# Score matmuls of an attention and gated-MLP block in runs of 16, with a new order of all steps

## The chip, the cores and the metric

The kernel runs on one core of a Trainium2 chip. The metric is the device time of one execution in microseconds (us), as a median over several executions. Four engines compute: TensorE (PE) multiplies matrices into eight PSUM banks, VectorE (DVE) and ScalarE (ACT) work on elements, and GpSimd (POOL) here only prepares constants and issues some DMAs. SyncE (SP) issues most of the other DMAs.

## The reference, cut to what matters

The input x has 2048 rows of 512 elements, in bfloat16. The first half is attention with 32 heads of 16 elements, in which each row sees 8 earlier rows, 2 apart. The second half is a gated MLP of width 1376.

```python
q, k, v = split_heads(layernorm(x) @ wqkv)        # 32 heads of 16
idx = pos[:, None] - arange(8)[None, :] * 2       # 8 shifts: 0, 2, ..., 14
logits = einsum("bhsd,bhswd->bhsw", q, k[idx]) * 16 ** -0.5
logits = where(idx >= 0, logits, -1e9)
o = einsum("bhsw,bhswd->bhsd", softmax(logits), v[idx])
h = x + merge_heads(o) @ wo
n = layernorm(h)
return h + (relu(n @ W_gate) * (n @ W_up)) @ W_down
```

## The kernel before

**Chunks.** The 2048 rows are worked on in 4 chunks (`tk`) of 512 rows; a chunk is 4 blocks (`j`) of 128 rows. The 512 columns are 4 tiles (`t`) of 128. Lines are those of the kernel before.

**First norm and QKV.** `layernorm` takes the statistics on DVE (bn_stats, L393, and bn_aggr, L396), ACT works out 1/sqrt by Ln and Exp (L406, L410), and DVE writes the normalized row (L428). PE transposes it (L459), and a copy (L473 on ACT, for two blocks of chunk 0 L471 on DVE) puts it into a `quad` tile. Twelve groups of four matmuls (L505) per chunk make q, k and v in transposed form; ACT copies each group out of its bank (L513).

**Scores.** The 8 shifts are two halves (`hf`) of four. For a half, DVE multiplies q by four shifted views of k (L552), for two tiles t at a time: two products of 128 x 4096 per half, each in a `big` tile. PE then sums over the elements of a head with the constant matrix `sel` (L558). Such a matmul has 32 output rows, and four of them with different `tile_position` fill the 128 rows of one bank. A product gives 8 matmuls, and a half has two products, which add up in the same bank. ACT takes the exp of the bank (L574); in chunk 0 a mask follows (L577).

**Softmax sum and values.** L591 sums the two halves' exps, ACT makes the reciprocal by Ln and Exp (L594, L597). In chunks 1 to 3 the exps are scaled by it (L606); in chunk 0 the scaling comes at the end (L647). PE spreads each shift's weights over the head's rows with matmuls on 32 rows of the array (L619), and ACT copies the 8 banks into one `big` tile (L625). For each t DVE multiplies by the 8 shifted views of v (L640) and adds the shifts up: the first addition, of halves of 4 shifts, is a DMA with accumulation issued by POOL (L672) in chunks 0 to 2 and a DVE add in chunk 3; the rest are DVE adds (L643, L666).

**Output of attention and MLP.** L692 multiplies by wo, L703 adds the residual on DVE and sums the row, L363 on ACT gives the sum of squares of the second norm, which ends as the first does. The MLP goes by 11 groups of 128 columns: up and gate (L730), copies out by ACT (L734, L737), product on DVE (L750). L767 multiplies by W_down, L778 adds the residual on DVE, and L782 on SP stores the result.

**Order.** Every step is an `Op` with an engine, an estimated duration, the steps that it depends on, buffers and a priority. `Plan.order` places the steps one after the other: of the steps that can start soonest on an engine, it takes the one with the lowest `prio`, and it gives out the buffers too (8 PSUM `bank`s, 9 `quad`, 5 `big`, 5 `row`, 2 `up_sb`, 2 `gr` and others). The priority comes from the list `RANK`, by the number of the step in the order of creation. The order that results is written into the program, and each engine works through its own queue of instructions in that order. `MERGE` is the tuple of chunks whose score matmuls of one half make one step. `DMAT` names norms that are transposed by DMA, `LNA` those whose normalized row is written on ACT; the first is empty, the second all zeros.

Of the kernel before, what the change touches and what calls it, by code (L numbers as in the profile page):

```python
# [8 lines left out]
P = 128  # L9
# [6 lines left out]


RANK = [
    0, 1, 2, 3, 4, 5, 6, 7, 8, 9, 10, 11, 12, 13, 14, 15, 18, 17, 19, 22,
    25, 30, 34, 37, 27, 32, 38, 21, 24, 28, 31, 33, 36, 40, 16, 20, 23, 26, 29, 35,  # L20
    39, 42, 44, 48, 53, 43, 51, 56, 41, 62, 67, 54, 55, 64, 77, 84, 46, 50, 65, 71,
    73, 76, 89, 92, 93, 97, 75, 79, 69, 74, 85, 99, 96, 119, 123, 128, 72, 94, 82, 102,
    105, 108, 141, 154, 158, 135, 147, 139, 153, 143, 116, 130, 120, 126, 134, 165, 175, 213, 215, 219,
    157, 167, 199, 217, 238, 174, 185, 230, 234, 240, 184, 194, 227, 233, 236, 245, 250, 243, 247, 248,
    254, 251, 258, 261, 265, 253, 255, 262, 268, 263, 270, 274, 277, 281, 288, 285, 291, 293, 287, 292,
    282, 294, 296, 310, 318, 319, 326, 302, 306, 330, 335, 346, 325, 352, 334, 337, 342, 354, 307, 328,
    362, 313, 321, 361, 365, 316, 323, 338, 369, 373, 353, 374, 355, 358, 344, 372, 336, 350, 378, 371,
    377, 357, 382, 380, 387, 349, 379, 390, 363, 388, 375, 385, 366, 408, 417, 421, 424, 437, 442, 467,
    472, 419, 495, 498, 501, 384, 429, 470, 476, 52, 59, 47, 60, 45, 57, 49, 58, 63, 70, 83,
    91, 81, 88, 95, 80, 86, 78, 87, 90, 107, 117, 100, 103, 104, 109, 98, 101, 136, 151, 166,  # L30
    173, 127, 137, 131, 171, 155, 168, 152, 156, 163, 169, 122, 132, 129, 203, 150, 216, 222, 149, 221,
    160, 235, 241, 246, 249, 252, 257, 298, 266, 278, 283, 275, 272, 305, 308, 314, 311, 312, 339, 347,
    376, 381, 317, 327, 356, 359, 324, 333, 360, 368, 332, 340, 364, 370, 392, 399, 389, 393, 401, 406,
    404, 410, 403, 407, 398, 402, 409, 412, 413, 416, 420, 423, 426, 433, 430, 436, 439, 428, 431, 432,
    435, 438, 473, 480, 481, 496, 461, 468, 488, 499, 502, 448, 451, 444, 449, 443, 445, 453, 457, 459,
    465, 471, 456, 464, 458, 463, 486, 489, 493, 505, 414, 477, 483, 490, 394, 450, 455, 511, 497, 523,
    520, 540, 500, 515, 546, 550, 553, 492, 504, 503, 506, 508, 541, 562, 573, 576, 538, 564, 578, 583,
    531, 567, 575, 580, 548, 565, 587, 590, 66, 110, 68, 111, 106, 112, 61, 113, 115, 133, 145, 162,
    138, 144, 164, 140, 146, 142, 159, 161, 170, 176, 212, 220, 172, 178, 204, 207, 177, 180, 195, 201,
    218, 224, 200, 205, 182, 189, 179, 186, 191, 197, 188, 192, 242, 271, 284, 297, 320, 264, 289, 295,  # L40
    299, 304, 341, 343, 345, 383, 348, 415, 425, 422, 418, 427, 391, 395, 411, 400, 396, 434, 441, 462,
    466, 452, 460, 491, 494, 440, 447, 474, 478, 446, 454, 485, 487, 512, 518, 516, 524, 509, 514, 528,
    532, 521, 542, 527, 539, 522, 526, 535, 536, 544, 545, 549, 555, 551, 557, 560, 556, 561, 554, 558,
    563, 568, 569, 577, 584, 591, 595, 571, 574, 597, 598, 604, 618, 622, 621, 624, 596, 619, 626, 627,
    633, 606, 610, 623, 628, 593, 600, 642, 609, 613, 582, 588, 586, 592, 602, 607, 617, 645, 650, 637,
    643, 616, 620, 612, 630, 652, 547, 572, 552, 579, 585, 660, 665, 668, 672, 654, 674, 678, 681, 661,
    669, 673, 676, 648, 671, 675, 679, 114, 124, 118, 148, 125, 183, 121, 181, 187, 190, 198, 206, 193,
    208, 210, 196, 211, 202, 209, 214, 225, 229, 223, 226, 259, 280, 267, 290, 239, 244, 231, 237, 228,
    232, 276, 286, 256, 260, 273, 301, 269, 303, 279, 315, 309, 300, 322, 329, 331, 351, 386, 367, 397,
    405, 469, 475, 479, 482, 484, 507, 513, 519, 510, 517, 525, 533, 534, 530, 529, 566, 608, 611, 614,  # L50
    543, 570, 581, 601, 537, 594, 599, 603, 559, 589, 605, 615, 631, 636, 641, 647, 635, 639, 625, 629,
    638, 640, 649, 651, 644, 646, 632, 634, 653, 655, 657, 664, 658, 663, 666, 659, 667, 656, 662, 670,
    713, 718, 694, 699, 716, 720, 711, 715, 723, 709, 712, 701, 705, 687, 707, 708, 710, 714, 685, 688,
    689, 691, 696, 700, 680, 684, 703, 690, 693, 692, 695, 683, 686, 677, 682, 697, 698, 702, 704, 717,
    719, 724, 706, 721, 727, 725, 729, 722, 726, 730, 733, 739, 744, 749, 731, 735, 738, 743, 728, 734,
    736, 740, 742, 746, 747, 748, 732, 737, 741, 745,
]


# [33 lines left out]
class Plan:  # L93
# [9 lines left out]
    def add(self, key, *a, **k):  # L103
        op = Op(*a, **k)
        op.key = key
        op.seq = len(self.ops)
        if RANK:
            op.prio = RANK[op.seq]
        self.ops.append(op)
        for b in set(op.take) | set(op.use):  # L110
            b.left += 1
        return op
# [57 lines left out]
def kernel(  # L170
# [11 lines left out]
    nc = tc.nc  # L182
# [4 lines left out]
    NT = D // P  # L187
# [116 lines left out]
    add = plan.add  # L304
# [3 lines left out]

    DACC = tuple((k, t) for k in range(3) for t in range(4))
    DAL = 5.5  # L310
    NWARM = 48
    DMAT = ()

# [1 line left out]

    RPE, OPE = (), ()

    MERGE = ()

    BCN = 4  # L320

# [18 lines left out]
    def layernorm(tk, src, dst_slots, pr, groups, on_act, residual=None):  # L340
        ln = "h" if residual else "x"


        dst = Buf(dst_slots)
        mv, rs, nb = Buf(mv_s), Buf(rs_s), Buf(nb_s)
        sm, sq = (residual, Buf(sq_s)) if residual else (None, None)
        evs = []
        for grp in groups:
            ag, xns = [], {}
            gk = str(grp[0]) if len(groups) > 1 else ""  # L350
            lo, hi = grp[0], grp[-1] + 1
            for j in grp:
                if residual:
# [8 lines left out]
                    def f_sq(j=j, xn=xns[j], h=h):  # L362
# [4 lines left out]
                    a = add((ln + "nm" + gk, tk), "DVE", DSM, f_nm, [src[j][0]], pr, take=[mv], use=[sm], lat=DL)  # L367
                    ag.append(add((ln + "sq" + gk, tk), "ACT", A5 + 0.1 if h else 0.73, f_sq, [a], pr,
                                  take=[sq, xns[j]], use=[mv] + ([h] if h else []), lat=AL))
                elif tk == 0 and j == BPC - 1:  # L370
# [15 lines left out]
                    a = add(("xsu", tk), "ACT", 0.75, f_su, [src[j]], pr, take=[xns[j], sm], lat=AL)  # L386
                    a = add(("xnm", tk), "DVE", DSM, f_nm, [a], pr, take=[mv], use=[sm], lat=DL)
                    ag.append(add(("xsq", tk), "ACT", 0.75, f_sq, [a], pr, use=[mv, xns[j]], lat=AL))
                else:
# [8 lines left out]
                    a = add((ln + "st" + gk, tk), "DVE", DST, f_st, [src[j]], pr, take=[st], lat=DL)  # L398
# [40 lines left out]
            if (ln, tk) in DMAT:  # L439
                for j in range(lo, hi):  # L440
                    xn, a = norm(j)

                    def f_td(j=j, xn=xn):
                        for t in range(NT):
                            nc.sync.dma_start_transpose(out=dst.t[:, t, j * P:(j + 1) * P],
                                                        in_=xn.t[:, t * P:(t + 1) * P])

                    evs.append(add((ln + "td" + gk, tk), "SP", 2.0, f_td, [a], pr, take=[dst], use=[xn], lat=2.5))
                continue
            step = 1 if tk == 0 and not residual else 2  # L450
            for j0 in range(lo, hi, step):
                tp, ds, xs = Buf(tp_s), [], []
                for j in range(j0, min(j0 + step, hi)):
                    xn, a = norm(j)
# [33 lines left out]
    for tk in range(NCK):  # L488
# [10 lines left out]
        for n, (c, t) in enumerate(seq):  # L499
            mm = Buf(mm_s)  # L500
            pr = base + 10 + 0.1 * n
# [14 lines left out]
            if tk == 0 and n < 4:  # L516
# [4 lines left out]
                a = add(("qkv%d" % n, tk), "PE", 2 * MM, lambda f=f_mm, hs=hs: f(hs, CS), xev[2:] + [wl, e],  # L521
                        pr, take=[mm], use=[xnT], lat=PEL)
            else:
                a = add(("qkv%d" % n, tk), "PE", 4 * MM, f_mm, xev + [wl], pr, take=[mm], use=[xnT], lat=PEL)
# [13 lines left out]
        for hf in range(2):  # L538
            sc, ex = Buf(at_s), Buf(ex_s)
            scd, prd = [], []  # L540
            for t in range(0, NT, 2):
# [13 lines left out]
                def f_sc(t=t, sc=sc, pb=pb):  # L555
                    for u in range(2):
# [5 lines left out]
                a = add(("pr%d" % hf, tk), "DVE", D40, f_pr, [d[k] for k in (t, t + 1) for d in (qd, kd, kp)],  # L562
                        apr, take=[pb], use=[qT], lat=DL)
# [4 lines left out]
            else:  # L568
                for a, pb, f in prd:
                    scd.append(add(("sc%d" % hf, tk), "PE", 2 * MM + SW, f, [a] + scd[-1:], apr,  # L570
                                   take=[sc], use=[pb], lat=PEL))
# [8 lines left out]
            a = add(("ex%d" % hf, tk), "ACT", A5, f_ex, scd, apr, take=[ex], use=[sc], lat=AL)  # L580
            if tk == 0:
                a = add(("mk%d" % hf, tk), "DVE", DSM, f_mk, [a], apr, use=[ex], lat=DL)
# [29 lines left out]
        for w0 in range(0, W, BCN):  # L612
# [9 lines left out]
            a = add(("bc%d" % hf, tk), "PE", MM + SW, f_bc, [exd[hf]], apr + 1, take=bcs, use=[exs[hf]], lat=PEL)  # L622
# [9 lines left out]
        for t in range(NT):  # L632
# [13 lines left out]
            def f_om(t=t, mt=mt, rc=rc, OT=OT):  # L646
# [3 lines left out]
                    take=[mt], use=[ab], lat=DL)  # L650
# [36 lines left out]
        for j in range(BPC):  # L687
# [10 lines left out]
            def f_rs(j=j, od=od, sm=sm, tk=tk):  # L698
# [3 lines left out]
                else:  # L702
# [3 lines left out]
            a = add(("wo%d" % j, tk), "PE", (5 if tk in RPE else 4) * MM, f_wo, list(oev.values()) + [wload["o"]],  # L706
                    base + 50, take=[od], use=[OT], lat=PEL)
            if tk in RPE:
                a = add(("rs%d" % j, tk), "ACT", A5 + 0.1, f_rs, [a], base + 50, take=[sm], use=[od], lat=AL)
            else:  # L710
                a = add(("rs%d" % j, tk), "DVE", D5 + 0.1, f_rs, [a], base + 50, take=[sm], use=[od], lat=DL)
# [7 lines left out]
        for f0 in range(0, NFT, 2):  # L719
# [3 lines left out]
            for ft in fts:  # L723
                fs = P if ft < NFF else FTAIL
                um, gm = Buf(mm_s), Buf(mm_s)
                pr = mb + ft * 0.1
# [9 lines left out]
                def f_ge(gm=gm, gr=gr, fs=fs, i=ft - f0):  # L736
                    nc.scalar.activation(out=gr.t[:fs, i, :], in_=gm.t[:fs, :], func=ACT.Relu)  # L737

                a = add(("mm%d" % (f0 // 2), tk), "PE", 4 * MM, lambda f=f_mm, um=um: f(wu_sb, um), hev + [wload["u"]], pr,
                        take=[um], use=[hnT], lat=PEL)  # L740
# [19 lines left out]
        for n, (j, c0, c1) in enumerate(parts):  # L760
# [23 lines left out]
            a = None  # L784
# [50 lines left out]
```

## Time and profile before

| What | Value |
|---|---|
| Time, median of 11 executions | 207.7 us (206.54 to 208.26) |
| Profiled execution, its own time | 207.93 us |
| Its span, from first to last instruction | 206.2 us |
| Mean granted TensorE clock | 0.989 |
| PE busy | 197.2 us (96%), 1136 matmuls recorded |
| DVE busy | 155.2 us (75%) |
| ACT busy | 131.7 us (64%) |
| POOL busy | 12.3 us (6%) |
| Products for the scores, L552 | 16, mean 2277 ns |
| Multiplies by v, L640 | 16, mean 2280 ns |
| Score matmuls, L558 | 128 of 128 x 512, mean 379 ns each |

The profile describes a single execution, so durations and shares belong to the 206.2 us of its span. Tenths of busy time stand for 40 equal slices of the span, about 5.15 us each. In a timeline each row is a group of like instructions: start, length, engine, line, operation, and the written and read buffers; in square brackets stands idle time ahead of the row and what ended it. Matmul lengths overlap, so the time from one start to the next says what a matmul takes from the engine.

### The profile page before, as it was taken

Reading aid. Unit: us, or ns where it says so; the run is one execution under the profiler, and the core shown is the slowest. Engines: PE = TensorE matmul, PEld = TensorE weight load, DVE = VectorE, ACT = ScalarE, POOL = GpSimd, SP = SyncE. Lnnn points to the kernel's source line nnn. Section 1 sums busy time; section 2 is a strip of 40 time slices with the busy share of each in tenths; the row PEclk is TensorE's granted clock in tenths of the full one; section 3 lists DMA queues with packets and bytes.
Section 4 is the critical chain, followed back from the end, with each engine's and each line's share of the span. In section 5 each row is a group of like instructions: output and inputs, shape, how many; then the busy total and the mean of one; then the engine's idle time right before and its main releaser. Section 6 shows DMA issues by size and latency. Waiting matters only on the chain.

```text
span 206.2 us, 2989 instructions
## 1 busy us (share of the span) xinstructions
PE 197.2 (96%) x1136; PEld 96.9 (47%) x1155; DVE 155.2 (75%) x246; ACT 131.7 (64%) x257; POOL 12.3 (6%) x26
## 2 busy tenths in 40 slices
PE   8399999999999999999999999999999999999994
PEld 7265534555444434443454444454444445444452
DVE  6549999999999999998699855699994644021314
ACT  4537789978759994677945748935656823565500
POOL 3000000140000004100014000000000000000000
PEclk9969999999999999999999999999999999999999
DMA  5999900099000007930019910000300001100003
GB/s 151 338 373 406 339 33 5 18 192 196 4 0 0 3 0 149 195 64 3 2 49 192 208 48 16 0 0 3 102 0 0 0 3 40 61 0 0 3 0 102
DMA packets 10541, 16.99 MB, mean 82 GB/s; under 512 B 704, under 2 KB 7840, under 8 KB 10528
## 3 DMA queue, kind: packets, MB, share of 16 engines
q0 software_dynamic: 1728, 6.29, 16.2%
q1 hardware_dynamic: 7984, 9.73, 13.8%
q10 hardware_dynamic: 816, 0.79, 1.1%
q8 instruction: 9, 0.15, 0.3%
q14 instruction: 4, 0.03, 0.0%
HBM read 8.42 MB, written 2.10 MB: 51 GB/s over the span
## 4 chain that ended last, share of the span: by engine, by line
PE 64%; DVE 23%; DMA 5%; ACT 2%; issue 2%; SPq 1%
PE bank L730 37%; PE bank L767 18%; DVE big L552 11%; PE bank L692 5%; DMA x_sm<-in_A_x_dram 5%; DVE big L640 3%; DVE row L428 2%; DVE st L393 2%; DVE big L643 2%; PE bank L558 1%; PE bank L459 1%; ACT big L625 1%; DVE x_sm L703 1%; PE bank L619 1%; DVE quad L647 1%
## 5 line engine op out<-in xcount | busy, mean ns | idle before, releaser
L730 PE MATMUL bank<-quad,wu_sb 128*128 128x512 bf16 (+1 forms) x173 | 42.7, 379 | 0.2
L730 PE MATMUL bank<-quad,wg_sb 128*128 128x512 bf16 (+1 forms) x171 | 41.8, 379 | 0.3
L767 PE MATMUL bank<-wd_sb,gT 128*128 128x512 bf16 (+3 forms) x183 | 39.7, 366 | 0.2
L737 ACT ACTIVATE gr<-bank 128x512 bf16<-128x512 f32 (+1 forms) x44 | 25.8, 607 | 18.0 <-PE bank L730 12.6
L552 DVE TENSOR_TENSOR big<-quad,kT 128x4096 bf16<-128x4096 bf16 x16 | 36.1, 2277 | 0.0
L640 DVE TENSOR_TENSOR big<-big,vT 128x4096 bf16<-128x4096 bf16 x16 | 35.7, 2280 | 0.3 <-ACT big L625 0.3
L734 ACT CAST up_sb<-bank 128x512 bf16<-128x512 f32 (+1 forms) x44 | 25.6, 599 | 12.8 <-PE bank L730 8.9
L750 DVE TENSOR_TENSOR gT<-gr,up_sb 128x1024 bf16<-128x1024 bf16 (+1 forms) x24 | 15.3, 642 | 21.3 <-ACT up_sb L734 12.2
L730 PEld LDWEIGHTS <-wu_sb 128*128 128x128 bf16 (+1 forms) x176 | 17.4, 100 | 21.0 <-issue 1.3
L730 PEld LDWEIGHTS <-wg_sb 128*128 128x128 bf16 (+1 forms) x176 | 17.5, 100 | 20.6 <-issue 0.7
L767 PEld LDWEIGHTS <-gT 128*128 128x128 bf16 (+1 forms) x187 | 18.0, 98 | 18.9 <-issue 0.2
L473 ACT COPY quad<-bank 128x1024 bf16<-128x1024 bf16 (+1 forms) x16 | 14.7, 963 | 10.2 <-PE bank L459 10.2
L778 DVE TENSOR_TENSOR row<-x_sm,bank 128x512 bf16<-128x512 bf16 (+1 forms) x17 | 10.6, 652 | 13.8 <-PE bank L767 13.8
L625 ACT CAST big<-bank 128x512 bf16<-128x512 f32 x32 | 17.6, 608 | 1.7 <-PE bank L619 1.5
L505 PE MATMUL bank<-quad,wq_sb 128*128 128x512 bf16 (+1 forms) x72 | 16.8, 370 | 1.8 <-DMA wq_sb<-in_A_wqkv_dram 1.8
L643 DVE TENSOR_TENSOR big<-big 128x1024 bf16<-128x1024 bf16 (+2 forms) x24 | 17.0, 727 | 1.3 <-DMA big<-big 1.3
L505 PE MATMUL bank<-quad,wk_sb 128*128 128x512 bf16 (+1 forms) x70 | 16.9, 371 | 0.3 <-issue 0.2
L672 POOL DMA_DIRECT2D big<-big x12 | 10.5, 872 | 100.8 <-DVE big L640 76.1
L505 PE MATMUL bank<-quad,wv_sb 128*128 128x512 bf16 x61 | 15.3, 379 | 0.3 <-issue 0.2
L692 PE MATMUL bank<-wo_sb,quad 128*128 128x512 bf16 x62 | 15.2, 380 | 0.1
L513 ACT CAST kT<-bank 128x512 bf16<-128x512 f32 x16 | 9.3, 597 | 7.9 <-PE bank L505 7.6
L703 DVE SCALAR_TENSOR_TENSOR x_sm<-x_sm,bank 128x512 bf16<-128x512 bf16 x16 | 10.8, 682 | 3.7 <-PE bank L692 3.7
(65 smaller groups left out, 165.3 us busy)
## 6 DMA issues: line engine op xcount, KB each, us to landing
big<-big POOLq DMA_DIRECT2D x12, 512.0 KB, 5.7
out_dram<-row SPq DMA_DIRECT2D x15, 128.0 KB, 1.7
x_sm<-in_A_x_dram SPq DMA_DIRECT2D x3, 512.0 KB, 10.9
wu_sb<-in_B_W_up_dram SPq DMA_DIRECT2D x1, 1376.0 KB, 10.6
wg_sb<-in_B_W_gate_dram SPq DMA_DIRECT2D x1, 1376.0 KB, 13.6
wd_sb<-in_B_W_down_dram SPq DMA_DIRECT2D x1, 1280.0 KB, 15.5
wq_sb<-in_A_wqkv_dram SPq DMA_DIRECT2D x1, 512.0 KB, 8.2
wk_sb<-in_A_wqkv_dram ACTq DMA_DIRECT2D x1, 512.0 KB, 8.7
```

Of the source, the lines that this page charges most:

```text
L473: nc.scalar.copy(out=o, in_=i)
L505: nc.tensor.matmul(mm.t[:, lo:hi], lhsT=w3_sb[c][:, dt, t:D:NT], rhs=xnT.t[:, dt, lo:hi], start=(dt == 0), stop=(dt == NT - 1))
L552: V.tensor_tensor(out=pb.t[:].rearrange("p (t w) s -> p t w s", t=2), in0=q4, in1=k4, op=ALU.mult)
L625: nc.scalar.copy(out=ab.t[:, w, :], in_=bc.t[:])
L640: V.tensor_tensor(out=mt.t[:], in0=ab.t[:], in1=v8, op=ALU.mult)
L643: V.tensor_tensor(out=mt.t[:, 0:n, :], in0=mt.t[:, 0:n, :], in1=mt.t[:, n:2 * n, :], op=ALU.add)
L692: nc.tensor.matmul(od.t[:], lhsT=OT.t[:, t, j * P:(j + 1) * P], rhs=wo_sb[:, t, :], start=(t == 0), stop=(t == NT - 1 and tk not in RPE))
L730: nc.tensor.matmul(mm.t[:fs, :], lhsT=w_sb[:, dt, ft * P: ft * P + fs], rhs=hnT.t[:, dt, :], start=(dt == 0), stop=(dt == NT - 1))
L734: nc.scalar.copy(out=ub.t[:fs, i, :], in_=um.t[:fs, :])
L737: nc.scalar.activation(out=gr.t[:fs, i, :], in_=gm.t[:fs, :], func=ACT.Relu)
L750: V.tensor_tensor(out=gt.t[:fs, 0:n, :], in0=gr.t[:fs, 0:n, :], in1=ub.t[:fs, 0:n, :], op=ALU.mult)
L767: nc.tensor.matmul(od.t[:, c0:c1], lhsT=gts[ft].t[:fs, ft % 2, j * P:(j + 1) * P], rhs=wd_sb[:fs, ft, c0:c1], start=(ft == 0), stop=(ft == ...
```

## The change

In each chunk, the score matmuls of one half become one step of 16 matmuls that waits for both products of the half, where there were two steps of 8 that each waited for one. There are 8 steps fewer, and the list of ranks has 742 numbers in place of 750. All numbers in it are new, so the order of the steps on every engine and the buffers that they get change too. A transpose by DMA is rewritten with two new duration constants; since `DMAT` is empty, it belongs to code that is not reached. `LNA` is not edited: all normalized rows are written on DVE.

```diff
 RANK = [
-    0, 1, 2, 3, 4, 5, 6, 7, 8, 9, 10, 11, 12, 13, 14, 15, 18, 17, 19, 22,
...
-    736, 740, 742, 746, 747, 748, 732, 737, 741, 745,
+    1, 3, 4, 2, 0, 5, 56, 6, 7, 41, 155, 205, 184, 248, 716, 8, 11, 10, 12, 14,
...
+    723, 738,
 ]
...
     DAL = 5.5
+    TDD, TDL = 2.4, 1.6
     NWARM = 48
     DMAT = ()
...
-    MERGE = ()
+    MERGE = (0, 1, 2, 3)
...
                     def f_td(j=j, xn=xn):
-                        for t in range(NT):
-                            nc.sync.dma_start_transpose(out=dst.t[:, t, j * P:(j + 1) * P],
-                                                        in_=xn.t[:, t * P:(t + 1) * P])
+                        nc.sync.dma_start_transpose(out=dst.t[:, :, j * P:(j + 1) * P], in_=xn.t[:])
 
-                    evs.append(add((ln + "td" + gk, tk), "SP", 2.0, f_td, [a], pr, take=[dst], use=[xn], lat=2.5))
+                    evs.append(add((ln + "td" + gk, tk), "SP", TDD, f_td, [a], pr, take=[dst], use=[xn], lat=TDL))
```

These lines stand in both kernels; with `MERGE` filled, the first branch is taken:

```python
            if tk in MERGE:
                scd = [add(("sc%d" % hf, tk), "PE", 4 * MM + SW, lambda p=prd: [f() for _, _, f in p],
                           [a for a, _, _ in prd], apr, take=[sc], use=[b for _, b, _ in prd], lat=PEL)]
            else:
                for a, pb, f in prd:
                    scd.append(add(("sc%d" % hf, tk), "PE", 2 * MM + SW, f, [a] + scd[-1:], apr,
                                   take=[sc], use=[pb], lat=PEL))
```

## The prediction

> **What bounds it now.** I read the engines' tenths first, then the chain of waits, then TensorE's (PE's) timeline, then four stretches from PE's first large matmul to its last.
>
> ```profile
> PE   8399999999999999999999999999999999999994
> ...
> DVE  6549999999999999998699855699994644021314
> ...
> PEclk9969999999999999999999999999999999999999
> ```
>
> ```profile
> 9.87:20.40 10.53, 10.31 (x56) 6.55 (x57) 7.44 (x15) 5.30 (x11) 0.00 (x0) 0.84 1.05 387
> 20.40:70.34 49.94, 49.12 (x341) 23.96 (x345) 49.91 (x71) 41.79 (x80) 3.59 (x4) 1.00 0.34 83
> 70.34:130.42 60.08, 59.71 (x317) 26.22 (x321) 51.41 (x72) 42.24 (x85) 6.88 (x8) 1.00 0.40 80
> 130.42:203.30 72.88, 72.51 (x366) 35.24 (x370) 39.67 (x65) 37.51 (x71) 0.00 (x0) 1.00 0.06 19
> ```
>
> The columns of the second fence are stretch, length, then busy time of PE, weight loads, DVE, ACT, POOL, clock, DMA. PE is full from 9.87 us on. DVE is full too from 20.4 to 70.3 (49.91 of 49.94 us), which is why the chain follows DVE up to 69.75 us and PE alone afterwards. A busy PE may still be badly used, so I look at when its matmuls start:
>
> ```profile
> 67.31 1.07 PE L459 MATMUL bank<-identity,row 128*128 128x128 bf16 x16
> 68.31 1.05 PE L558 MATMUL bank<-big,sel 128*32 128x512 bf16 x16
> 69.79 0.61 PE L558 MATMUL bank<-big,sel 128*32 128x512 bf16 x8 [0.43 <-DVE big L552]
> 70.34 1.04 PE L730 MATMUL bank<-quad,wu_sb 128*128 128x512 bf16 x3
> ...
> 72.51 2.75 PE L730 MATMUL bank<-quad,wu_sb 128*128 128x512 bf16 x12
> 75.10 1.03 PE L730 MATMUL bank<-quad,wg_sb 128*128 128x512 bf16 x4
> 76.05 0.62 PE L558 MATMUL bank<-big,sel 128*32 128x512 bf16 x8
> 76.60 1.04 PE L730 MATMUL bank<-quad,wu_sb 128*128 128x512 bf16 x4
> 77.57 0.61 PE L558 MATMUL bank<-big,sel 128*32 128x512 bf16 x8
> ```
>
> Each row starts with start and length in us. Twelve matmuls of 512 columns take 75.10 - 72.51 = 2.59 us, 0.216 each. The four before a score run (L558) take 76.05 - 75.10 = 0.95 instead of 0.86: going into the run costs 0.09 to 0.10. A score run of 8 is two passes of four concurrent matmuls, 0.43 us, but holds PE 76.60 - 76.05 = 0.55: 0.10 for leaving and 0.02 because the four don't start together. The rows at 68.31 and 69.79 show the only clear stall on DVE: the first 16 need about 0.97 us (1.05, less the 0.38 of a matmul's own length, gives the last start; 0.31 more to the next matmul), but the next eight start 1.48 later. About 0.5 to 0.6 us is lost.
>
> The whole PE time can be added up. Matmuls of 512 columns: 765 x 0.216 = 165.1; of 256: 54 x 0.1085 = 5.9; transposes 128 x 0.056 = 7.1; scores 128 x 0.054 = 6.9; broadcasts (L619) 32 x 0.054 = 1.7; together 186.8 us. The stretch is 193.4. The 6.6 us over are 1.7 of half clock near 10.6 to 14.0 us, 43 changes between full matmuls or transposes, scores and broadcasts at 0.096 (4.1), the stall above, and rounding. So almost nothing but half clock and changes can be won on PE.
>
> **The skill.** The Trainium skill, "TensorEngine Tiling (Array Packing)", Key Properties, says that changing the tiling mode drains TensorE. It gives no price; the 0.096 us is the trace's. "TensorE: Matmul & The Clock Gate", Part 2, says matmuls stay in program order and only weight loads are pulled ahead: a run that waits holds up everything behind it, as at 69.79. The same page, Part 1, describes a half clock after an idle window of 3.4 us; the trace has it (clock 0.84 in the first stretch). What leads to it (the wait for wq's DMA, 1.79 us) is untouched here. "Perfetto Trace Analysis", opening note, says matmul busy time misleads because matmuls overlap: a row says 379 ns for a matmul that costs 216.
>
> **The change, part by part.** Several edits issue nothing: DMAT is empty in both, so the new transpose by DMA and TDD/TDL do not occur, and LNA is zero in both, so all 32 norms (L428) stay on DVE as before. Every engine gets the same instructions. Only their order differs, and the scores stand in 8 runs of 16.
>
> 1. Changes of mode. By the two orders, before has 13 entries into scores from full matmuls or transposes, 14 exits to these, 8 entries into broadcasts, 7 exits and one broadcast-to-score change: 43. After has 8 + 6, 6 + 8, and two score-to-broadcast changes: 30. Saved: 13 x 0.096 = 1.25 us, plus 6 fewer groups x 0.02 = 0.1. All of it lies on PE, which is full: **-1.35 us**. Were a waiting DVE or ACT always last there, it would be worth 0; it can't be more than eight joins of 0.2. I keep 0 to -1.6.
>
> 2. The stall at 69 us. Before, PE had run out of QKV filler at 66.8 and met unfinished products. In the new order chunk 0's products and sums come earlier on DVE, and its score runs and projection stand between QKV groups that still remain. I follow both queues with the prices of the timeline (DVE from start to start: product L552 or multiply L640 2.20, norm 0.325, bn_stats 0.60, add of 1024 0.60, 512-wide 0.34, residual 0.60; ACT copy 0.48, transpose copy 0.91). PE asks / DVE has it, in us: first scores 22.9 / 22.6; second 27.5 / 27.0; chunk 0's projection (L692) 53.1 / 53.0; third scores 56.5 / 51.7; fourth 61.9 / 60.1; transposes of h 63.0 / 62.6; fifth 66.1 / 65.8; first up/gate 67.1 / 66.9 (ACT's copy); sixth 71.0 / 70.5; chunk 1's projection 93.3 / 93.0; chunk 2's 125.1 / 123.1. No long stall is left: -0.6. But many margins are 0.1 to 0.5 us, on queues where a late one moves all behind it. I charge **+0.35** for new stalls, from 0 to 2. Net **-0.25**.
>
> 3. The wait that merging adds. The first eight matmuls of a half now wait for its second product, and then come in front of the exp: product to exp grows by 16 minus 8, about 0.42 us, eight times. Queued behind the waiting run on PE are QKV or up/gate groups; behind the exp are the broadcasts, ACT's eight copies and L640. Where DVE has a backlog it is covered: DVE had no idle time from 20.4 to 70.3. Without that cover it is up to 8 x 0.42 = 3.4 us. I take 0, since the walk above already has the longer run in it; 0.4 of DVE idle before the first L640 (near 34 us) is its only visible trace.
>
> 4. POOL's queue. The accumulating DMAs (L672) keep their order behind the multiplies.
>
> ```profile
> DVE big L643 <- DMA big<-big: 1.3, 1, 1.3
> ```
>
> Before, the last one of chunk 2 was late: multiply ended at about 112.2, add started at 119.72, 7.5 us. In the new order chunk 2's four multiplies end near 109.5 to 116.2 and the adds stand 7.6, 7.0, 6.6 and 6.0 us later, so they may slip by 0.4 to 1.5 us; the projection has 2.0 us to spare. Cost 0, at most 0.3. In chunks 0 and 1 adds come 7 to 9 us later. SP's queue has the same 15 + 2 output writes, each behind its L778; nothing waits on them but row buffers. The tail (last half-width add 0.42 us, then the write) is the same.
>
> Sum: -1.35 - 0.25 = **-1.6 us**. The profiled execution took 207.93 (span 206.2 and 1.7 around it), giving 206.3; the median shown is 0.2 lower: 206.1.
>
> **The rivals.**
> - Earlier PE, same DVE (no change). DVE's work is as large as before, and DVE is full to 70 us and 86% busy to 130. If the order makes PE wait for DVE by what it saves, the end stays: 207.7, within 0.3. For it: margins of 0.1 to 0.5 us. Against it: after 70 us the chain is PE alone, and by my walk up/gate of chunk 0 starts at 67.1 instead of 70.3, with only 1.5 us of PE work (two scores, a broadcast) pushed behind it.
> - Exposed exps (slower). Step 3 surfaces: in the merged halves the exp comes late and broadcasts, copies and L640 follow late, so DVE idles and then holds PE at L692 and at the transposes. Each exposed half costs 0.42 us. It decides from more than 1.6 / 0.42, about four of the eight halves. With all eight it is -1.6 + 3.4 = +1.8: 209.5; with six, 208.6. For it: both halves of a chunk need ACT at once (29 to 36 us, ACT has no gap in my walk). Against it: ACT idles elsewhere (64% busy), and DVE has chunks of other work queued.
> - The runs do not stay together on the chip, or the drain is paid inside a run as well: then step 1 is 0 and only the stall goes, 207.4. The x16 at 68.31, two neighbouring runs in one pass of starts, speaks against it.
>
> **How the numbers follow.** A difference of 0.3% is 0.6 us, about what a measurement of this kernel can tell from no change. The forecast, 206.1 with 205.1 to 207.0 of its own (steps 1 and 2 at their ends without a long stall), has 0.79. No change by waiting PE has 0.06 and the drain rival 0.03 (207.4, within 0.3%); exposed exps have 0.12. That makes faster 0.79, same 0.09, slower 0.12. The range reaches up to 207.6 to leave out little more than the slower rival, and down to 205.1.
>
> **What would show it.** Right: 8 score rows of x16, each from start to next start near 0.97; no idle over 0.3 us on PE after 10 us but at the named margins; up/gate (L730's line) of chunk 0 starting at 67 to 68 us; PE's stretch from first wq matmul to last L767 of 191.8 instead of 193.4. Wrong: gaps before scores or L692 with releaser DVE adding up to over 1.6 us; DVE idle of several us before L640; score rows broken up; a second half-clock stretch.

## The result, and the profile after

The changed kernel takes **205.35 us** as a median of 12 executions (204.5 to 206.14); the kernel before, run beside it 47 times, takes 207.72 (206.54 to 208.51). The ratio is 0.9886, with a 95% interval from 0.9871 to 0.9901: 2.4 us are gone. The profiled execution took 205.19 us with a span of 203.4. In the profile after, the product is L551 (it was L552), the scores L557 (L558), the multiply by v L639 (L640), the projection L691 (L692), up and gate L729 (L730), W_down L766 (L767).

The tenths of DVE and of the TensorE clock, and the chain of waits by engine:

```profile
DVE  6559999999999999999659978699993662211314
PEclk9999999999999999999999999999999999999999
...
PE 78%; DVE 12%; DMA 5%; issue 2%; SPq 1%
```

DVE is as solid as before up to some 95 us; what has changed is who sets the end. Before, the chain gave PE 64% and DVE 23% and followed DVE to 69.75 us. Now it follows PE from 20.07 to 32.6, DVE from there to 52.57, where the last sum for chunk 0's projection is ready, and then PE. The half clock near 10 us is missing in this execution, which needs care and is taken up below.

The same four stretches (stretch, length, busy time of PE, weight loads, DVE, ACT, POOL, clock, DMA), cut at the first large matmul, the first scores, the first up/gate and a start of W_down matmuls near 130 us:

```profile
9.43:22.35 12.92, 11.49 (x79) 7.78 (x81) 9.75 (x17) 7.65 (x15) 0.00 (x0) 1.00 1.06 384
22.35:66.64 44.29, 43.99 (x296) 22.43 (x300) 43.99 (x65) 36.74 (x74) 3.59 (x4) 1.00 0.34 75
66.64:130.92 64.28, 63.91 (x352) 28.37 (x356) 56.75 (x81) 46.88 (x96) 6.88 (x8) 1.00 0.37 74
130.92:200.50 69.58, 69.21 (x353) 33.80 (x356) 37.78 (x60) 34.72 (x62) 0.00 (x0) 1.00 0.06 20
```

From the first large matmul to the first up/gate PE now needs 66.64 - 9.43 = 57.21 us, where it needed 70.34 - 9.87 = 60.47: **3.26 us less**. From there to the end of the matmuls of L766 (L767 before) it needs 133.71 instead of 132.74 us: **0.97 more** (the last matmul is counted at the 0.11 us that one of 256 columns takes). Ten of the sixteen groups of 8 score matmuls stand ahead of the first up/gate and no longer twelve, and two of the 8 broadcasts and no longer three, so this work was pushed behind. At 0.054 us for each of its 20 matmuls it is 1.08 us, and one change between kinds of matmuls fewer stands there (17 instead of 18). Together PE's stretch is 193.21 before and 190.92 after, **2.29 us shorter**, and PE itself starts 0.44 earlier in this execution.

PE's timeline around the place where the kernel before stalled:

```profile
61.53 1.05 PE L557 MATMUL bank<-big,sel 128*32 128x512 bf16 x16
62.51 0.62 PE L458 MATMUL bank<-identity,row 128*128 128x128 bf16 x8
...
65.66 1.05 PE L557 MATMUL bank<-big,sel 128*32 128x512 bf16 x16
66.64 1.04 PE L729 MATMUL bank<-quad,wg_sb 128*128 128x512 bf16 x3
...
70.63 1.05 PE L557 MATMUL bank<-big,sel 128*32 128x512 bf16 x16
71.61 0.39 PE L618 MATMUL bank<-ex,spread 32*128 32x512 bf16 x4
```

Each score run holds all 16 matmuls and takes 62.51 - 61.53 = 0.98 us to the next start, and no row carries a wait. The transposes of h start at 62.51 instead of 67.31. Their rows come from DVE, here first before and then after:

```profile
61.76 4.48 DVE L552 TENSOR_TENSOR big<-quad,kT 128x4096 bf16<-128x4096 bf16 x2
66.16 1.37 DVE L428 TENSOR_SCALAR row<-x_sm,mv,rs 128x512 bf16<-128x512 bf16 x4
```

```profile
57.35 4.48 DVE L551 TENSOR_TENSOR big<-quad,kT 128x4096 bf16<-128x4096 bf16 x2
61.75 1.38 DVE L429 TENSOR_SCALAR row<-x_sm,mv,rs 128x512 bf16<-128x512 bf16 x4
63.05 4.49 DVE L551 TENSOR_TENSOR big<-quad,kT 128x4096 bf16<-128x4096 bf16 x2
```

The norm of h stands 4.4 us earlier: DVE has made 9 products for the scores by then and not 11. Two products of 2.2 us each went behind the norm; they feed scores that PE takes later, the last of them between up/gate groups.

One thing is new and was not foreseen. Between 17.5 and 20.3 us PE waits for rows of chunk 1's first norm:

```profile
19.43 0.40 PE L458 MATMUL bank<-identity,row 128*128 128x128 bf16 x4 [1.13 <-DVE row L429]
20.07 0.40 PE L458 MATMUL bank<-identity,row 128*128 128x128 bf16 x4 [0.25 <-DVE row L429]
```

With what a matmul's modelled length hides, some 1.5 us are lost. Before, this stretch lost 1.7 us to half clock.

### The profile page after: what moved, and what is told of

It reads as the page before. It is cut to its first block, busy times and chain, and to the rows that moved or that the text cites. A ratio compares the mean times of both kernels' runs of the same rounds, so it can differ in the third digit from the quotient of the medians.

```text
span 203.4 us, 3004 instructions
## 1 busy us (share of the span) xinstructions
PE 194.2 (95%) x1134; PEld 97.3 (48%) x1155; DVE 154.9 (76%) x246; ACT 130.9 (64%) x257; POOL 12.3 (6%) x26
## 4 chain that ended last, share of the span: by engine, by line
PE 78%; DVE 12%; DMA 5%; issue 2%; SPq 1%
PE bank L729 37%; PE bank L766 19%; PE bank L504 7%; PE bank L691 7%; DMA x_sm<-in_A_x_dram 5%; PE bank L557 4%; DVE big L639 3%; DVE big L551 3%; PE bank L458 2%; DVE big L642 2%; DVE st L394 2%; PE bank L618 1%; DVE row L429 1%; DVE quad L646 1%; PE bank L590 1%
## 5 line engine op out<-in xcount | busy, mean ns | idle before, releaser
L729 PE MATMUL bank<-quad,wu_sb 128*128 128x512 bf16 (+1 forms) x174 | 42.0, 379 | 0.3
L729 PE MATMUL bank<-quad,wg_sb 128*128 128x512 bf16 (+1 forms) x170 | 41.6, 379 | 0.2
L766 PE MATMUL bank<-wd_sb,gT 128*128 128x512 bf16 (+3 forms) x183 | 40.0, 366 | 0.2
L639 DVE TENSOR_TENSOR big<-big,vT 128x4096 bf16<-128x4096 bf16 x16 | 35.7, 2284 | 1.5 <-ACT big L624 1.5
L551 DVE TENSOR_TENSOR big<-quad,kT 128x4096 bf16<-128x4096 bf16 x16 | 36.1, 2282 | 0.0
L729 PEld LDWEIGHTS <-wg_sb 128*128 128x128 bf16 (+1 forms) x176 | 17.4, 100 | 20.7 <-issue 1.1
L729 PEld LDWEIGHTS <-wu_sb 128*128 128x128 bf16 (+1 forms) x176 | 17.5, 100 | 20.4 <-issue 0.2
L766 PEld LDWEIGHTS <-gT 128*128 128x128 bf16 (+1 forms) x187 | 17.9, 98 | 19.0 <-issue 0.7
L472 ACT COPY quad<-bank 128x1024 bf16<-128x1024 bf16 (+1 forms) x16 | 15.2, 972 | 7.4 <-PE bank L458 7.3
L624 ACT CAST big<-bank 128x512 bf16<-128x512 f32 x32 | 16.6, 610 | 1.2 <-PE bank L618 1.2
L504 PE MATMUL bank<-quad,wq_sb 128*128 128x512 bf16 (+1 forms) x69 | 15.9, 355 | 1.4 <-DMA wq_sb<-in_A_wqkv_dram 1.3
L364 ACT ACTIVATE row<-x_sm,mv 128x512 bf16<-128x512 bf16 x16 | 11.4, 712 | 8.6 <-DVE mv L356 8.5
L504 PE MATMUL bank<-quad,wk_sb 128*128 128x512 bf16 (+1 forms) x71 | 16.4, 355 | 0.1
L691 PE MATMUL bank<-wo_sb,quad 128*128 128x512 bf16 x62 | 14.5, 379 | 0.2
L394 DVE BATCH_NORM_STATS2 st<-x_sm 128x6 f32<-128x512 bf16 x15 | 9.6, 676 | 4.6 <-DMA x_sm<-in_A_x_dram 4.6
```

What stands on the lines that cost most here:

```text
L472: nc.scalar.copy(out=o, in_=i)
L504: nc.tensor.matmul(mm.t[:, lo:hi], lhsT=w3_sb[c][:, dt, t:D:NT], rhs=xnT.t[:, dt, lo:hi], start=(dt == 0), stop=(dt == NT - 1))
L551: V.tensor_tensor(out=pb.t[:].rearrange("p (t w) s -> p t w s", t=2), in0=q4, in1=k4, op=ALU.mult)
L624: nc.scalar.copy(out=ab.t[:, w, :], in_=bc.t[:])
L639: V.tensor_tensor(out=mt.t[:], in0=ab.t[:], in1=v8, op=ALU.mult)
L691: nc.tensor.matmul(od.t[:], lhsT=OT.t[:, t, j * P:(j + 1) * P], rhs=wo_sb[:, t, :], start=(t == 0), stop=(t == NT - 1 and tk not in RPE))
```

## The experiments

The theories are named by letters in what was expected. **A**: the merging saves changes of tiling mode (from matmuls on the full array to those on parts of it, the 128x32 of the scores or the 32x128 of the broadcasts, or back) at about 0.1 us each, on a PE that is the bound. **B**: the new order alone brings the gain, by removing the stall on DVE at 69 us, and the merging nothing. **C**: the missing half clock made the difference. **D**: the old list of ranks does not suit merged runs, whatever the buffers do; **A+** says that the old ranks fail only because buffers are held too long. Executions of one kernel spread over 1 to 4 us, so for a finer reading I also compare traces by the time from the first statistics of chunk 1 (which start when its x has landed, the head of the chain in most of them) to the end of the span: 193.19 us before, 190.80 after.

**1. Merging alone, with the old ranks.**

```diff
-            op.prio = RANK[op.seq]
+            self.skip += key is not None and key[0] in ("sc0", "sc1")
+            op.prio = RANK[op.seq + self.skip]
...
-    MERGE = ()
+    MERGE = (0, 1, 2, 3)
```

> The old ranks with the score matmuls merged (the first of the two old ranks of each half is dropped), so the merge alone. PE changes its tiling mode 29 times instead of 43. Theory A (changes of mode cost PE 0.096 us each, and PE is full): 14 x 0.096 + 0.1 = 1.4 us less than the kernel before, about 206.3 us, a little more if the first halves now wait for their second product, a little less if the stall near 69 us goes. Theory B (only the new order counts, the drains lie beside other waits): 207.7 us as before.

Measured: 214.26 us, ratio 1.0331 (1.0296 to 1.0365): 6.75 us slower than before. Both expectations missed. It has 14 changes of mode fewer, and loses far more elsewhere. DVE's timeline (the product is L553 here, the multiply L641):

```profile
30.62 2.28 DVE L553 TENSOR_TENSOR big<-quad,kT 128x4096 bf16<-128x4096 bf16 x1
...
34.21 2.25 DVE L553 TENSOR_TENSOR big<-quad,kT 128x4096 bf16<-128x4096 bf16 x1
36.39 4.48 DVE L641 TENSOR_TENSOR big<-big,vT 128x4096 bf16<-128x4096 bf16 x2
...
45.29 2.29 DVE L641 TENSOR_TENSOR big<-big,vT 128x4096 bf16<-128x4096 bf16 x1
...
49.13 2.29 DVE L641 TENSOR_TENSOR big<-big,vT 128x4096 bf16<-128x4096 bf16 x1
```

The two products of chunk 1 made at 30.62 and 34.21 are first halves of merged runs, whose second products come only later; the runs start at 55.39 and 59.95. Two of the five `big` tiles are held until then, and the four multiplies of chunk 0, which need one each, come in pieces to 51.4 us. (Experiment 8 asks how much of the loss comes from this.) Chunk 0's projection starts at 61.81 us and not at 56.29. Then PE meets the merged runs before their products are there:

```profile
66.98 0.62 PE L559 MATMUL bank<-big,sel 128*32 128x512 bf16 x8
71.32 1.04 PE L559 MATMUL bank<-big,sel 128*32 128x512 bf16 x8 [3.72 <-DVE big L553]
72.30 1.89 PE L460 MATMUL bank<-identity,row 128*128 128x128 bf16 x16
```

Half a run stands at 66.98, its other half waits 3.72 us in the middle of the run, and after this gap the transposes take 1.82 us instead of 0.89: the granted clock is 0.50 from 70.9 to 74.3. This is the wait of the prediction's step 3, at a size that it had no price for.

**2. The new order without merging.** Both runs of a half get the rank of the merged step.

```diff
-            op.prio = RANK[op.seq]
+            self.skip += key is not None and key in self.seen and key[0] in ("sc0", "sc1")
+            self.seen.add(key)
+            op.prio = RANK[op.seq - self.skip]
...
-    MERGE = (0, 1, 2, 3)
+    MERGE = ()
```

> The new ranks with two score runs of 8 per half as before, both with the merged step's rank, so the new order alone. 40 changes of mode instead of 30. Theory A: 10 x 0.096 + 0.1 = about 1.1 us more than the changed kernel, about 206.4 us, and still about 1.3 below the kernel before. Theory B: 205.35 us, as the changed kernel.

Measured: 207.82 us, ratio to before 1.0003 (0.9982 to 1.0023). The new order without merging is worth nothing, so B falls. A's figure, 206.4, was missed as well, by 1.4 us. The stall at 69 us is gone here too: from the first large matmul to the first up/gate PE needs 58.23 us (before 60.47, after 57.21), but from there to its end 135.45 (132.74 and 133.71). From the landing of x the trace needs 193.42 us, 2.62 more than after. Its 10 more changes of mode are worth about 1.1 of it (at the 0.109 of experiments 3 and 4). Most of the rest is one stall ahead of chunk 1's first up/gate (L731 here):

```profile
105.19 0.59 PE L592 MATMUL bank<-ex,same 128*128 128x512 bf16 x2
106.92 1.89 PE L731 MATMUL bank<-quad,wg_sb 128*128 128x512 bf16 x8 [1.14 <-ACT quad L474]
```

The start comes 1.73 us after the one before, for two matmuls that need 0.43: 1.3 us. Splitting the runs also let the planner place other steps differently (on DVE and ACT as well), so this was more than one change, and the run doesn't say what the same order without this stall would have brought.

**3 and 4. A run broken in the middle, and its control.** Experiment 3 puts one full-array matmul of 64 columns, with zeros, between the two halves of each run; experiment 4 puts four tiled ones there, at the tile positions of the scores, and so leaves the mode alone. The order is that of the kernel after.

```diff
+                def f_z(sc=sc):
+                    nc.tensor.matmul(sc.t[:, 0:64], lhsT=warm[:], rhs=warm[:, 0:64], start=False, stop=False)
```

```diff
+                def f_z(sc=sc):
+                    for g in range(4):
+                        nc.tensor.matmul(sc.t[g * HB:(g + 1) * HB, 0:64], lhsT=warm[:, 0:HB], rhs=warm[:, 0:64],
+                                         start=False, stop=False, tile_position=(0, g * HB))
```

> The changed kernel with one matmul of zeros over the full array (128 rows, 64 columns) between the two halves of each run of 16: it adds zero to the bank and two changes of mode, 16 in all. Theory A: 16 x 0.096 plus 8 x 0.05 for the matmul itself and the second stagger, 1.9 us more: 207.2 us. Theory B: the same as the next run, which adds as much work and no change of mode.

> Control for the run with a full-array matmul of zeros: four matmuls of zeros of 64 columns at the four tile positions of the score matmuls stand between the halves, so as much array time, but no change of mode. Both theories: 8 x 0.03 to 0.05, that is 0.2 to 0.4 us more than the changed kernel, 205.6 to 205.8 us. If it costs as much as the other, not the mode but the interruption is what counts.

Measured: 207.25 us for the full matmul (ratio to before 0.9974, 0.9952 to 0.9996) and 204.34 for the control (0.9863, 0.9818 to 0.9908). One run in PE's timeline, with the full matmul (L566) and then with the tiled ones (L567):

```profile
21.54 0.62 PE L557 MATMUL bank<-big,sel 128*32 128x512 bf16 x8
22.09 0.20 PE L566 MATMUL bank<-warm 128*128 128x64 bf16 x1
22.22 0.62 PE L557 MATMUL bank<-big,sel 128*32 128x512 bf16 x8
22.77 1.49 PE L504 MATMUL bank<-quad,wq_sb 128*128 128x512 bf16 x6
```

```profile
20.85 0.62 PE L557 MATMUL bank<-big,sel 128*32 128x512 bf16 x8
21.29 0.20 PE L567 MATMUL bank<-warm 128*32 128x64 bf16 x4
21.32 0.61 PE L557 MATMUL bank<-big,sel 128*32 128x512 bf16 x8
21.86 1.49 PE L504 MATMUL bank<-quad,wq_sb 128*128 128x512 bf16 x6
```

The broken run takes 22.77 - 21.54 = 1.23 us, the control 1.01, the plain run 0.98: 0.11 us for each of the two added changes. By the landing of x the spans are 192.73 and 190.98; 1.75 us over 16 changes is **0.109 us each**, and it all reaches the end. From the first scores to PE's last matmul the two traces differ by the same 1.75 (180.08 and 178.34). So A holds for the kernel after: a change of mode is on the path. The executions at full clock point the same way: 206.54 us with the full matmul, 204.34 with the tiled ones, 205.05 after. The control's median lies below what either theory expected. In its trace x landed early (11.11 us, 12.60 in the trace after), which is the likely reason; for its other executions the landing isn't known. By the landing it is 0.18 us slower than after, for eight times 0.03 that its runs are longer.

**5. The kernel after once more**, beside 6 and 7.

> The changed kernel once more, beside the next three on the same chip. In the profiles so far, first work on the second chunk of x starts between 11.1 and 13.0 us, as its DMA lands, and the spread of a kernel's times is of that size. Both theories: a time near 205.35 us, and from the first statistics of chunk 1 to the end of the span 190.8 us as in the profile after (before: 193.2).

Measured: 204.95 us (204.45 to 205.36), ratio 0.9858 (0.9832 to 0.9883); by the landing of x 190.80, the same as in the first trace. The chain of waits is PE's for 89% here and for 78% there, with the same order of steps: between 32.6 and 52.57 us PE and DVE are so close that the chain can take either.

**6 and 7. Is it the half clock?** 24 matmuls of 128 columns on the tile `warm` stand in the first groups, to keep the clock up: in the kernel before (6) and in the kernel after (7).

```diff
+            if op.key == ("qkh0", 0):
+                for _ in range(24):
+                    nc.tensor.matmul(op.take[0].t[:, 0:P], lhsT=warm[:], rhs=warm[:], start=True, stop=True)
```

> The kernel before with 24 more warming matmuls of 128 columns on PE between the first transposes and the first matmul with wq, where PE waits for wq's DMA, so that the clock is not halved afterwards. Theory A (DVE sets the pace of both kernels until the first up/gate group, so that the half clock at 10.6 to 14.0 us is hidden): within 0.4 us of the kernel before, and from the first statistics of chunk 1 to the end 193 us. Theory C (the half clock, 1.7 us of loss in the profile before and absent in the profile after, is a large part of the gain): 1.5 to 1.7 us less than before, near 206.0.

> The changed kernel with the same 24 warming matmuls. Theory A: within 0.4 us of the changed kernel, since without the half clock PE only waits longer at 18 to 20 us for the rows of chunk 1's norm. Theory C: no change either, as the profile after has no half clock; with the run before it this separates the two.

Measured: 207.65 us for the kernel before with them (ratio 0.9998, 0.9978 to 1.0019), and 205.89 for the kernel after with them (0.9878, 0.9833 to 0.9923), too spread over six executions (203.72 to 206.84) for a fine answer. The trace of 6 has no half clock, and nothing moved: first scores 10.51 us after the first large matmul, where it was 10.53, and 193.21 us from the landing of x, where it was 193.19. But the 24 matmuls stood between two groups, not ahead of the first as was expected, and took 1.34 us of PE themselves (10.43 to 11.77), so this swaps one loss for another and does not say by itself what the half clock costs. The rows of 6:

```profile
9.16 0.63 PE L505 MATMUL bank<-quad,wq_sb 128*128 128x256 bf16 x4 [0.92 <-DMA wq_sb<-in_A_wqkv_dram]
...
10.43 1.50 PE L800 MATMUL bank<-warm 128*128 128x128 bf16 x24
...
19.67 0.61 PE L558 MATMUL bank<-big,sel 128*32 128x512 bf16 x8
```

Its executions at full clock take 207.22 us, and those of the kernel before 207.37 (table below): about 1.3 us of PE work ahead of the first scores is free, or nearly so, in the kernel before. In the trace of 7 the 24 matmuls took 1.34 us as well (12.55 to 13.89), the wait at 18 to 20 us was gone, and PE's stretch was 190.64 us against 190.92. But x landed early there (10.48 us), which alone could take the wait away, so 7 stays inconclusive. From the landing it needs 191.46 us, 0.66 more than after: with so early a landing the time from it is no longer the measure.

What the half clock costs is read from the executions, sorted by granted clock:

| Kernel | Clock 0.998 to 1.0 | Clock 0.989 to 0.992 |
|---|---|---|
| before | 207.37 us (41) | 207.83 us (26) |
| after | 205.05 us (12) | 205.46 us (5) |
| after with full matmuls (3) | 206.54 us (11) | 207.49 us (10) |
| before with 24 matmuls (6) | 207.22 us (13) | 208.35 us (8) |

Means, with the number of executions in brackets: before those beside the experiments, after those of its first measurement and of experiment 5. Before has 3 more and after 1 more near 0.983, experiment 3 one at 208.96 and 6 one at 208.95. One window of half clock (3.4 us at 0.5, or 1.7 of 206 us, hence 0.992) goes with 0.4 to 0.5 us in the kernels before and after, 0.9 in experiment 3 and 1.1 in 6, where the 24 matmuls come on top, and in none of these with 1.7. (In experiment 7 it is 1.9, between three executions and two: too few to count.) Whether the clock itself costs this, or a late DMA that goes with it, isn't shown. At equal clock the change is worth 207.37 - 205.05 = **2.3 us**, so C falls. At full clock experiment 2 stands at 207.47 us (19 executions), as before.

**8. Experiment 1 with the buffers freed.** Chunk 1's products may be placed only after the last multiply of chunk 0.

```diff
-                        [d[k] for k in (t, t + 1) for d in (qd, kd, kp)]
+                        [d[k] for k in (t, t + 1) for d in (qd, kd, kp)] + ([last_mu] if tk == 1 else [])
...
+            last_mu = m
```

> Old ranks, merged, and in the planner alone chunk 1's products for the scores placed after the last multiply by v of chunk 0. In the run with old ranks and the merge, two products of chunk 1 were made at 30 and 34 us and held two of the five big buffers until their merged run at 55 and 60 us, so two multiplies of chunk 0 came 8 and 10 us later than the first two. Theory A+ (the merge costs buffers, and an order that keeps a half's products together gets the gain of the drains back): the four multiplies stand together, L692's line starts near 53 to 57 us instead of 61.8, and the time falls from 214.3 by 5 to 8 us, to 206.3 to 209. Theory D (the old ranks are bad for the merge in other ways, above all in the later chunks): over 211 us.

Measured: 213.32 us, ratio 1.0267 (1.0236 to 1.0299), 0.9 less than in experiment 1. A+ falls, with the 5 to 8 us that it forecast. The four multiplies now stand together, but four products come between the additions that follow:

```profile
35.62 8.90 DVE L641 TENSOR_TENSOR big<-big,vT 128x4096 bf16<-128x4096 bf16 x4 [2.56 <-issue]
44.55 2.29 DVE L553 TENSOR_TENSOR big<-quad,kT 128x4096 bf16<-128x4096 bf16 x1
...
50.57 2.29 DVE L553 TENSOR_TENSOR big<-quad,kT 128x4096 bf16<-128x4096 bf16 x1
...
55.18 2.29 DVE L553 TENSOR_TENSOR big<-quad,kT 128x4096 bf16<-128x4096 bf16 x1
...
57.84 2.29 DVE L553 TENSOR_TENSOR big<-quad,kT 128x4096 bf16<-128x4096 bf16 x1
```

Chunk 0's projection starts at 61.68, as late as in experiment 1. The edit has a price of its own: DVE idles 2.56 us ahead of the multiplies, where it made products in experiment 1. So what the held buffers alone cost there isn't shown. Score runs wait for products again:

```profile
70.14 1.05 PE L559 MATMUL bank<-big,sel 128*32 128x512 bf16 x16 [1.79 <-DVE big L553]
72.34 1.04 PE L559 MATMUL bank<-big,sel 128*32 128x512 bf16 x8 [1.16 <-DVE big L553]
```

This is what D expects: the order of products, multiplies and additions on DVE has to suit runs that wait for two products. How the 5.6 us over the kernel before divide between the late projection, these waits and the half clock from 71.3 to 78.1 is not settled. No experiment points to a kernel that is faster than the one after; its remaining wait, at 18 to 20 us, is for the norm of x's second chunk, which its DMA starts.

## Why the prediction was right

The forecast was 206.1 us, the measurement 205.35. It was inside the range, and the direction and most of the mechanism were right. Small slips in the sum of PE's time (765 x 0.216 is 165.2, and the total 186.9) don't touch it. Of its signs, the eight rows of x16 came as said; up/gate came at 66.64 us, a little ahead of its 67 to 68, and the wait of 1.13 us at 18 us was not among the margins that it named.

- **Step 1, changes of mode.** Right in size for the kernel after: 0.096 us read from start to start before, 0.109 by experiments 3 and 4. Runs of x16 with 0.98 us to the next start were as foreseen, so the drain rival is out. What was loose is "all of it lies on PE, which is full". In the kernel before, the chain ran along DVE to 69.75 us, and experiment 6 put 1.3 us of PE work ahead of the first scores at no cost: a full PE was not proof that every saving there counts. That it counts in the kernel after is shown by experiment 3. Why it does there is read from the traces: the new order brought chunk 0's norm of h forward on DVE, so that PE no longer meets DVE at 69 us. Of the 13 changes saved, 12 lie ahead of the first up/gate.
- **Step 2, the stall at 69 us.** Gone, as foreseen. The walk through both queues held in its differences: first scores 22.35 us for 22.9, projection of chunk 0 52.56 for 53.1, third scores 56.11 for 56.5, up/gate 66.64 for 67.1, chunk 1's projection 92.89 for 93.3. All are 0.4 to 0.6 early, and PE's start was 0.44 early (9.43 for 9.87). From the start to the first up/gate it gave 67.1 - 9.87 = 57.2, and 57.21 came. This agreement has luck in it: the walk carried the half clock of the trace before (1.7 us), and what came was the wait for chunk 1's norm (1.5 us).
- **The mis-sized term** is the +0.35 for new stalls. Apart from that wait no row of PE's timeline carries idle time from 20.5 us to the last matmul; gaps and rounding together changed by about -0.1. The miss lies behind the first up/gate: the sum had PE lose 1.6 us there (3.2 gained up to it, 1.6 in all), and it lost 0.97. The two scores and the broadcast pushed behind were priced at 1.5 us with changes of their own; in runs of 16 they brought none, and cost 1.0. PE's stretch then divides into about -1.4 for changes of mode (13 at 0.109), -0.6 for the stall, -0.2 for the wait in place of the half clock, and -0.1: -2.3 in all, where -1.6 was forecast. The first of these is priced by experiments 3 and 4; the others are read from the two traces alone.
- **Step 3, the wait that merging adds.** Taken as 0, and 0 in this order. In experiment 1, with the old ranks, merging does make PE wait, but not as the rival had it: not eight waits of 0.42 us for exps, but one of 3.72 inside a run, and then half clock. The prediction did not price a `big` tile that is held until its partner's product is made; experiment 8 leaves open what that costs.
- **Step 4, POOL's DMAs.** Taken as 0; chunk 2's projection started at 124.66 us for a walk of 125.1, no later than PE asked.
- **The rivals.** "Earlier PE, same DVE" failed: in the trace after, the part of DVE's work that PE waits for stands ahead of the part that it doesn't wait for, and DVE's total is as before (154.9 us busy for 155.2). "Exposed exps" did not show. That merging could go wrong by an unfit order was real: alone it costs 6.75 us, the order alone brings nothing, and both together bring 2.4.

## What to carry to other kernels

Joining two steps that wait for different producers saves a fixed price per join, here up to two changes of tiling mode of 0.1 us (13 over eight joins). It also holds the first producer's buffer until the second is done, and puts the whole wait into the middle of an in-order queue. So the join and the order of the producers have to be changed together: here each alone brought nothing or a loss. When an engine is full, check by the chain which engine sets the end before counting a saving on it. Where work can be added to the full engine for nothing, don't count a saving there.

## What the runs showed of the hardware

- **Half clock after a window that wasn't idle.** The Trainium skill, "TensorE: Matmul & The Clock Gate", Part 1, puts the half clock after an idle window of 3.4 us. In experiment 1 it begins at 70.9 us, after 3.4 us in which PE was busy for 0.10, in agreement. In experiment 8 no wait is as long (1.79 and 1.16 us), yet the clock is 0.50 from 71.3 us on; in the 3.4 us ahead of that PE was busy for 1.49 us, 44%. The columns are as in the stretches above:

```profile
67.90:71.30 3.40, 1.49 (x24) 0.55 (x17) 3.40 (x2) 3.40 (x11) 0.00 (x0) 1.00 0.00 0
71.30:74.70 3.40, 2.36 (x22) 1.52 (x22) 3.40 (x7) 2.52 (x7) 0.00 (x0) 0.50 0.00 0
```

  The half clock in the trace before came the same way, not after an idle window as the prediction read it. PE was busy for 48% of the 3.4 us ahead:

```profile
7.21:10.62 3.41, 1.62 (x19) 1.12 (x17) 1.18 (x4) 1.07 (x2) 0.00 (x0) 1.00 1.05 356
10.62:14.03 3.41, 3.19 (x14) 1.82 (x13) 1.07 (x2) 0.21 (x1) 0.00 (x0) 0.50 1.09 364
```

  In the nine traces that record changes of the clock, a state lasts 3.41 us or a multiple of it (3.41, 6.83, 191.15). With windows counted in such steps, and busy time as the trace models it, the clock fell to half, ahead of PE's last matmuls, after windows with PE busy for 3%, 45%, 48%, 49% and 51%. It stayed full after every other one, down to 50% (experiment 6, from 3.74 us) and 52% (after, from 3.81 us). So the border lies near one half here. The window from 71.3 us in experiment 8, 69% busy at half clock, was still followed by another at half clock.

- **The landing of one input moves the whole kernel.** In ten traces the first statistics of chunk 1 start anywhere from 10.48 to 12.96 us, behind the DMA of its x. Two traces of the kernel after, 12.60 and 12.69, both have 190.80 us from there to the end; the control of experiment 4, with 11.11, has 190.98. Much of the spread between executions of one kernel is thus likely the spread of this DMA, though no single execution without a trace shows it.
- **A change of tiling mode** costs 0.096 to 0.109 us, whether the matmul that forces it is of 512 columns or of 64.
